# A causal convolution feeding a gated feed-forward layer: weights fetched in six equal slices of 256 columns, their second halves copied in another order, and the first convolution read out by ScalarE alone

## The chip, the cores and the metric

The kernel runs on one core of a Trainium2 chip. The metric is the device time of one execution in microseconds (us). Every line number below is one of the kernel before, as its profile has them, unless the text says otherwise.

## The reference, cut to what matters

```python
# lightweight convolution: x is (8, 4096, 192), weight is (8, 7)
w = softmax(weight, axis=-1)                  # one row of 7 taps per head
x_pad = concat([zeros((8, 6, 192)), x], axis=1)
attn[b, s, 24*h + g] = sum_k w[h, k] * x_pad[b, s + k, 24*h + g]
# gated feed-forward layer over 32768 tokens
t = attn.reshape(32768, 192)
out = (maximum(t @ w_gate, 0) * (t @ w_val)) @ w_out   # 192 -> 1536 -> 192
```

Inputs and output are fp32; the kernel works in fp16 with fp32 sums.

## The kernel before, in words

**Two streams on the two halves of the array.** The eight batches are taken as two streams of four. Channels are cut into three chunks of 64 (`c` = 0 to 2), and partitions 0 to 63 hold a chunk of stream 0, partitions 64 to 127 the same chunk of stream 1. A matrix product of the first layer is therefore issued as pairs of 64-row matmuls on the two row halves of TensorE (L539). This needs each weight matrix twice: `Wg` and `Wv` (gate and value, 192 by 1536) lie in partitions 0 to 63, and again in 64 to 127. DMA brings the first copy, in column slices named by `CUTS` (L156): slice 0 has 128 columns, slices 1 to 4 have 256, slice 5 has 384. An on-chip copy on VectorE or GpSimd makes the second (L168, L177). "f0" to "f11" below are the twelve blocks of 128 columns of the first layer, in the order in which `gate_val` takes them.

**Units.** Sixteen units of 1024 tokens of each stream, `u` = 0 to 15. A unit has two windows of 512. For each window and each f, `gate_val` issues twelve matmuls (gate and value, three chunks, two streams), ScalarE writes the rectified gate (L550, tile `gr`), and VectorE multiplies it by the value out of PSUM (L551, tile `hT`). Then `project` multiplies by `Wo` (L568; L617 at the end), ScalarE and sometimes VectorE copy the result out of PSUM (L594), and SP stores it.

**Where the convolution comes from.** For later units, GpSimd, ScalarE and VectorE compute it beside TensorE, from tiles that GpSimd loads and rearranges (`lane_load` L199, `lane_turn` L463) and SP transposes (L467). At the very start there is no time for that. There, TensorE computes it with band matrices (`conv_dense`, L361): 120 small matmuls for window 0 of unit 0 (`first_block`, before f0) and 120 for window 1 (`second_block`, called between f4 and f5 of window 0). The results go from PSUM into the fp16 tile `xc`, which is the moving operand of L539. In `first_block`, ScalarE copies chunks 0 and 1 and VectorE copies chunk 2 (L379).

**What sets the order of the work.** Nothing is scheduled automatically: each engine runs its instructions in program order, and a semaphore wait holds everything behind it on that engine. GpSimd issues the loads of the first microseconds as well as its copies, all in one order: the first tokens (L125, L126), slices 0, 1 and 2 (each gate, then value), the tokens of window 1 (L87, tile `x_h`, one DMA per stream), slice 3, the copy of slice 2 (gate whole, value in two parts), slice 4, the gate part of slice 5, the copy of slice 3, the value part of slice 5, the copy of slice 4, `Wo` (L695), the copy of slice 5, and then the lane's loads. VectorE copies slice 0 at the beginning of `first_block` and slice 1 behind the chunk that it reads out. PSUM is handed out in four tiles of two banks in rotation. A new pair for f can start only when the pair of f-2 has been read by L550 and L551.

For f0 alone the twelve matmuls run chunk by chunk (gate and value of chunk 0, then of chunk 1, then of chunk 2); every other f takes all of the gate first.

Of the kernel before, what the change touches and what calls it, by code (L numbers as in the profile page):

```python
# [16 lines left out]
def kernel(  # L17
# [12 lines left out]
    nc = tc.nc  # L30
# [4 lines left out]
    DFF = moe_w_gate.shape[1]  # L35
    PAD = KW - 1
    NB = B // 2
    NCH = D // 64
    NBLK = D // 32
    NFF = DFF // 128  # L40
    WIN = 512
# [33 lines left out]
    def load_x(g):  # L75


        bp, toks = GROUPS[g]
        n, rows, step = len(toks), SUB if g < 2 else 128, toks[1] - toks[0]
        xt = xts[g] = xpool.tile([128, GSUB, 2, D], F16, name="x_h")  # L80
        for st in range(2):
            src = bass.AP(
                tensor=x.tensor,
                offset=x.offset + ((bp + NB * st) * S + toks[0] - PAD) * D,
                ap=[[D, rows], [step * D, n], [1, D]],
            )
            nc.gpsimd.dma_start(out=xt[0:rows, 0:n, st, :], in_=src)  # L87
            yield

    def load_rest(steps):  # L90
        for _ in steps:
            pass
# [11 lines left out]
    def stage(p0, rows, st, n_st, jj, n):  # L104
        at = room[p0 : p0 + rows, 0, 0, 0:1]
        dims = [[D * GSUB, n_st], [D, n], [1, D]]
        return bass.AP(
            tensor=at.tensor,
            offset=at.offset + D * (GSUB * st + jj),
            ap=[at.ap[0]] + [d for d in dims if d[1] > 1],  # L110
        )
# [3 lines left out]
    def body(st):  # L115
# [11 lines left out]
        out=xts[0][PAD : PAD + FIRST, 0, :, :],  # L127
        in_=bass.AP(
            tensor=x.tensor, offset=x.offset, ap=[[D, FIRST], [NB * S * D, 2], [1, D]]
        ),  # L130
# [22 lines left out]
    Wg = const.tile([128, NCH, DFF], F16)  # L153
    Wv = const.tile([128, NCH, DFF], F16)
    Wo = const.tile([128, NFF, D], F16)
    CUTS = [0, 128, 384, 640, 896, 1152, DFF]  # L156

    def load_w(s, which=3):
        cols = slice(CUTS[s], CUTS[s + 1])
        for src, dst in ((moe_w_gate, Wg), (moe_w_val, Wv))[which == 2 : 1 + (which > 1)]:  # L160
            nc.gpsimd.dma_start(
                out=dst[0:64, :, cols],
                in_=src.rearrange("(c p) f -> p c f", p=64)[:, :, cols],
            )

    def both_halves(copy, s, dst):
        cols = slice(CUTS[s], CUTS[s + 1])
        copy(out=dst[64:128, :, cols], in_=dst[0:64, :, cols])  # L168

    def pool_halves(s):  # L170
        both_halves(nc.gpsimd.tensor_copy, s, Wg)
        both_halves(nc.gpsimd.tensor_copy, s, Wv)

    def pool_parts(s):
        both_halves(nc.gpsimd.tensor_copy, s, Wg)
        for f0 in range(CUTS[s], CUTS[s + 1], 128):
            nc.gpsimd.tensor_copy(out=Wv[64:128, :, f0 : f0 + 128], in_=Wv[0:64, :, f0 : f0 + 128])  # L177

    xes, xrs, accs, prods = {}, {}, {}, {}

# [6 lines left out]
    def lane_load(v, hold=None):  # L187
# [4 lines left out]
        for j0, n, t in pieces(v):  # L192
# [4 lines left out]
            for st in range(2):  # L197
# [16 lines left out]
                    )  # L214
                yield

    load_w(0)
    load_w(1)
    load_w(2)
    load_rest(load_x(1))  # L220
    load_w(3)
    pool_parts(2)
    load_w(4)
    load_w(5, 1)
    pool_halves(3)
    load_w(5, 2)

    ex = const.tile([H, KW + 1], FP)
    nc.vector.memset(ex[:, KW : KW + 1], 1e-9)
# [21 lines left out]
    with nc.allow_low_precision("zero and one"):  # L251
        nc.vector.tensor_tensor(
            out=same[:], in0=col[:, 0:SEG], in1=s_of[:].to_broadcast([SUB, SEG]), op=ALU.is_equal
        )
        nc.vector.tensor_scalar(
            out=places[:, SUB - SEG : SUB - SEG + NROW],
# [7 lines left out]
        out=mx[:], in_=wr[:], axis=mybir.AxisListType.X, op=ALU.max, negate=True  # L264
# [6 lines left out]
    with nc.allow_low_precision("rounded as the band is"):  # L271
        nc.vector.tensor_scalar(
            out=soft[:],
# [7 lines left out]
        out=spread[0:SUB, 0, 0:H],  # L281
# [7 lines left out]
    with nc.allow_low_precision("products with one and zero"):  # L289
        nc.vector.tensor_tensor(  # L290
            out=diag[:],
# [6 lines left out]
    for a in range(2):  # L298
        for b in range(NSEG):
            nc.tensor.matmul(  # L300
                out=(bps, spread)[a][:, a, HB * SEG * b : HB * SEG * (b + 1)],
# [9 lines left out]
    for cols in (slice(0, 64), slice(64, D)):  # L311
        nc.scalar.copy(
            out=xts[0][0:ROWS0, 1:GSUB, 0, cols],
            in_=stage(0, ROWS0, 0, 1, 1, GSUB - 1)[:, :, cols],
# [25 lines left out]
    xc = {}  # L340
# [3 lines left out]
    def conv_dense(g, c, ps, bank):  # L344


        xt = xts[g]
        toks = GROUPS[g][1]
        t0 = toks[0]
        ends = toks[1:] + [t0 + WIN]  # L350
        for jj in (1, 2, 3, 4, 0):
            col, n = toks[jj] - t0, ends[jj] - toks[jj]
            rows = n + PAD
            for second in range(2):
                for st in range(2):
                    for k2 in range(2):
                        k = 2 * c + k2
                        h0, h1 = 32 * k // G, (32 * k + 31) // G
                        h, m = (h0, G * h1 - 32 * k) if second else (h1, 32)
                        p0 = 64 * st + 32 * k2  # L360
                        nc.tensor.matmul(  # L361
                            out=ps[p0 : p0 + m, bank, col : col + n],
                            lhsT=xt[0:rows, jj, st, 32 * k : 32 * k + m],
                            rhs=band(h)[0:rows, 0:n],
                            start=True,
                            stop=True,
                            tile_position=(0, p0),
                            skip_group_check=True,
                        )

    def first_block():
        xc[0] = xcpool.tile([128, NCH, UNIT], F16, name="xc")
        both_halves(nc.vector.tensor_copy, 0, Wg)
        both_halves(nc.vector.tensor_copy, 0, Wv)
        for c in range(NCH):
            ps = psum.tile([128, 2, 512], FP, name="ps")
            conv_dense(0, c, ps, 0)
            copy = nc.vector.tensor_copy if c == 2 else nc.scalar.copy
            copy(out=xc[0][:, c, 0:WIN], in_=ps[:, 0, :])  # L379

    def second_block():
        two, one = [psum.tile([128, 2, 512], FP, name="ps") for _ in range(2)]
        conv_dense(1, 0, two, 0)
        conv_dense(1, 1, two, 1)
        nc.scalar.copy(out=xc[0][:, 0:2, WIN : 2 * WIN], in_=two[:])
        conv_dense(1, 2, one, 0)
        nc.vector.tensor_copy(out=xc[0][:, 2, WIN : 2 * WIN], in_=one[:, 0, :])
# [138 lines left out]
    def gate_val(u, w):  # L526
        h = hpool.tile([128, NFF, 2, WIN], F16, name="hT")
        xcb = xc[u]
        for f in range(NFF):
            if u == 0 and w == 0 and f == 5:  # L530
                second_block()
            pss = [psum.tile([128, 2, 512], FP, name="ps") for _ in range(2)]
            order = [(i, c) for i in range(2) for c in range(NCH)]
            if u == 0 and w == 0 and f == 0:
                order = [(i, c) for c in range(NCH) for i in range(2)]
            for i, c in order:
                W = (Wg, Wv)[i]
                for st in range(2):
                    nc.tensor.matmul(  # L539
                        out=pss[i][:, st, :],  # L540
                        lhsT=W[64 * st : 64 * st + 64, c, 128 * f : 128 * (f + 1)],
                        rhs=xcb[64 * st : 64 * st + 64, c, WIN * w : WIN * (w + 1)],
                        start=(c == 0),
                        stop=(c == NCH - 1),
                        tile_position=(64 * st, 0),
                    )
            by_stream = u == 0 and w == 0 and f < 2
            for sts in (slice(0, 1), slice(1, 2)) if by_stream else (slice(0, 2),):
                gr = gpool.tile([128, 2, WIN], F16, name="gr")
                nc.scalar.activation(out=gr[:, sts], in_=pss[0][:, sts], func=ACTF.Relu)  # L550
                nc.vector.tensor_tensor(  # L551
                    out=h[:, f, sts], in0=gr[:, sts], in1=pss[1][:, sts], op=ALU.mult
                )
        return h
# [121 lines left out]


    first_block()
    taps = const.tile([H, KW], FP)
    nc.scalar.activation(taps[:], ex[:, 0:KW], ACTF.Copy, scale=sm[:])  # L680
    tap = const.tile([128, NCH, KW], FP)
    for h in range(H):
        r = G * h
        while r < G * (h + 1):
            c, n = r // 64, min(64 - r % 64, G * (h + 1) - r)
            nc.sync.dma_start(
                out=tap[r % 64 : r % 64 + n, c, :],
                in_=taps[h : h + 1, :].unsqueeze(1).to_broadcast([1, n, KW]),
            )
            r += n  # L690

    both_halves(nc.vector.tensor_copy, 1, Wg)
    both_halves(nc.vector.tensor_copy, 1, Wv)
    pool_halves(4)
    nc.gpsimd.dma_start(out=Wo[:], in_=moe_w_out.rearrange("(c p) d -> p c d", p=128))  # L695
    pool_halves(5)
    load_rest(lane_load(1))
    nc.gpsimd.tensor_copy(out=tap[64:128], in_=tap[0:64])
    load_rest(load_x(2))
# [3 lines left out]
    for u in range(NUNIT):  # L703
# [6 lines left out]
        if u == 0:  # L710
            hs.append(gate_val(0, 0))
# [10 lines left out]
        while len(hs) < 2:  # L722
            hs.append(gate_val(u, len(hs)))
# [45 lines left out]
```

## Time and profile before

| | us |
|---|---|
| median of 3 runs | 765.72 (765.51 to 765.99) |
| the profiled execution | 766.03 |
| its span, first to last instruction | 764.2 |
| TensorE busy in the span | 760.4 (99%) |
| VectorE, ScalarE, GpSimd busy | 705.7, 600.3, 378.8 |

How to read it: the profile page gives the busy time of each engine, and a chain of work followed back from the last instruction. Where the chain stays on one engine from end to end, that engine's own length is the time, and only its gaps can be taken away. PE is TensorE's matmuls, PEld its weight loads (which run ahead of the matmul that uses them), DVE is VectorE, ACT is ScalarE, POOL is GpSimd, SP the queue that issues the transposes and stores. In a timeline a row has the start, the time from the first to the last of the merged instructions, the engine, the line, the operation, what it writes and reads, and in brackets how long the engine sat idle before and what ended it. Matmuls of the two row halves overlap, so the time of one says less than the distance from one to the next.

### The profile page before, as it was taken

The page shows a single profiled execution, that of the slowest core. Times are in us where ns is not written, and L with a number is a line of the kernel's source. Part 1 is how long each engine was busy: PE and PEld are TensorE (multiplying, and loading weights), DVE is VectorE, ACT ScalarE, POOL GpSimd, SP SyncE. Part 2 cuts the span into 40 slices and gives each one's busy share as a digit, 9 for nine tenths or more (in the row PEclk, how much of TensorE's full clock was granted, in tenths as well). Part 3 has the DMA queues.
Part 4 walks back from the last instruction along what each step waited for, and adds up shares of the span by engine and source line. Part 5 has one row for each costly group of instructions (what it writes and reads, how often), then busy time and mean ns, then how long its engine had stood idle before and what let it go on. Part 6 is the DMA issues. An engine that isn't in the chain of part 4 may idle for free.

```text
span 764.2 us, 25118 instructions
## 1 busy us (share of the span) xinstructions
PE 760.4 (99%) x10935; PEld 518.6 (68%) x10935; DVE 705.7 (92%) x768; ACT 600.3 (79%) x733; POOL 378.8 (50%) x249
## 2 busy tenths in 40 slices
PE   9999999999999999999999999999999999999998
PEld 4495775957659576585866858567595775957658
DVE  7998999999999999999999999999999999999891
ACT  6787887878878787887878878787887887876571
POOL 8519448093571916629175390853909347090000
PEclk9999999999999999999999999999999999999999
DMA  9969037280442805529162281832818034220202
GB/s 117 130 111 145 7 97 79 65 114 22 95 64 84 95 24 109 46 85 95 32 113 36 85 94 44 107 29 90 88 44 130 8 98 60 64 49 16 70 1 84
DMA packets 131830, 55.93 MB, mean 73 GB/s; under 512 B 96584, under 2 KB 131720, under 8 KB 131720
## 3 DMA queue, kind: packets, MB, share of 16 engines
q1 hardware_dynamic: 90472, 38.66, 23.3%
q0 software_dynamic: 41104, 15.57, 20.6%
q8 instruction: 85, 1.39, 0.8%
q14 instruction: 25, 0.20, 0.1%
q10 hardware_dynamic: 144, 0.10, 0.0%
HBM read 31.48 MB, written 25.17 MB: 74 GB/s over the span
## 4 chain that ended last, share of the span: by engine, by line
PE 99%; ACT 0%; issue 0%
PE ps L539 65%; PE ps L568 32%; PE ps L617 1%; PE ps L145 0%; PE ps L361 0%; PE ps L300 0%; PE ps L402 0%; ACT acc L594 0%; PE ps L280 0%
## 5 line engine op out<-in xcount | busy, mean ns | idle before, releaser
L551 DVE TENSOR_TENSOR hT<-gr,ps 128x1024 f16<-128x1024 f16 (+1 forms) x386 | 469.1, 1216 | 36.2 <-ACT gr L550 9.4
L550 ACT ACTIVATE gr<-ps 128x1024 f16<-128x1024 f32 (+1 forms) x386 | 393.3, 1020 | 102.5 <-PE ps L539 100.6
L489 POOL TENSOR_TENSOR prods<-prods 128x1344 f32<-128x1344 f32 x70 | 212.3, 3032 | 289.8 <-DVE prods L485 286.4
L539 PE MATMUL ps<-xc,Wv 64*128 64x512 f16 x2304 | 316.6, 376 | 0.0
L539 PE MATMUL ps<-xc,Wg 64*128 64x512 f16 x2304 | 316.2, 376 | 0.0
L568 PE MATMUL ps<-Wo,hT 64*128 64x192 f16 x5952 | 248.8, 243 | 0.0
L568 PEld LDWEIGHTS <-hT 64*128 64x128 f16 x5952 | 246.4, 94 | 3.5
L539 PEld LDWEIGHTS <-Wv 64*128 64x128 f16 x2304 | 136.0, 94 | 113.4 <-POOL Wv L177 0.4
L539 PEld LDWEIGHTS <-Wg 64*128 64x128 f16 x2304 | 123.7, 94 | 121.4 <-issue 0.4
L513 DVE SCALAR_TENSOR_TENSOR acc<-x_r,tap,acc 128x576 f32<-128x576 f16 x225 | 165.3, 811 | 0.0
L483 ACT ACTIVATE prods<-x_r,tap 128x448 f32<-128x448 f16 x222 | 130.0, 660 | 0.0
L594 ACT COPY out_s<-ps 128x768 f32<-128x768 f32 (+1 forms) x64 | 45.6, 713 | 51.2 <-PE ps L568 39.8
L199 POOL DMA_DIRECT2D x_e<-in_x_dram x58 | 47.0, 822 | 15.3 <-ACT acc L499 11.5
L463 POOL COPY x_p<-x_e 128x960 f16<-128x960 f16 (+1 forms) x58 | 50.3, 907 | 0.7 <-DMA x_e<-in_x_dram 0.7
L489 POOL TENSOR_TENSOR xc<-prods 128x1344 f16<-128x1344 f32 x14 | 42.4, 3030 | 1.1
L513 DVE SCALAR_TENSOR_TENSOR xc<-x_r,tap,acc 128x576 f16<-128x576 f16 x45 | 34.1, 811 | 0.0
L499 ACT ACTIVATE acc<-x_r,tap 128x576 f32<-128x576 f16 x45 | 31.4, 763 | 0.0
L485 DVE TENSOR_SCALAR prods<-x_r,tap 128x448 f32<-128x448 f16 x70 | 26.6, 448 | 0.0
L594 DVE COPY out_s<-ps 128x384 f32<-128x384 f32 (+1 forms) x16 | 8.6, 540 | 11.5 <-PE ps L617 9.4
L617 PE MATMUL ps<-Wo,hT 128*128 128x192 f16 x96 | 8.1, 246 | 0.0
L617 PEld LDWEIGHTS <-hT 128*128 128x128 f16 x96 | 7.9, 98 | 0.2 <-issue 0.2
L145 PE MATMUL ps<-const-bfloat16-1.0 128*128 128x512 bf16 (+1 forms) x8 | 3.8, 609 | 0.8 <-PEq L753 0.8
(56 smaller groups left out, 55.9 us busy)
## 6 DMA issues: line engine op xcount, KB each, us to landing
out_dram<-out_s SPq DMA_DIRECT2D x62, 384.0 KB, 2.7
x_e<-in_x_dram POOLq DMA_DIRECT2D x34, 192.0 KB, 7.5
x_e<-in_x_dram POOLq DMA_DIRECT2D x24, 240.0 KB, 5.0
x_r<-x_p SPq DMA_TRANSPOSE x131, 4.7
Wo<-in_moe_w_out_dram POOLq DMA_DIRECT2D x1, 576.0 KB, 6.6
x_h<-in_x_dram POOLq DMA_DIRECT2D x2, 210.0 KB, 6.1
Wg<-in_moe_w_gate_dram POOLq DMA_DIRECT2D x4, 96.0 KB, 4.8
Wv<-in_moe_w_val_dram POOLq DMA_DIRECT2D x4, 96.0 KB, 5.8
```

The lines of the kernel that those rows point to most:

```text
L199: first = nc.gpsimd.dma_start(out=xe[:, j0 + start : j0 + n, st, :, :].rearrange("p j c r -> p j (c r)"), in_=bass.AP(tensor=x.tensor, off ...
L463: nc.gpsimd.tensor_copy(out=xp[:, j0 : j0 + n, :, st, :], in_=xe[:, j0 : j0 + n, st, :, :])
L483: engine.activation(out=out, in_=in_, func=ACTF.Copy, scale=scale)
L485: engine.tensor_scalar(out=out, in0=in_, scalar1=scale, scalar2=None, op0=ALU.mult)
L489: nc.gpsimd.tensor_tensor(out=pr[:, 0] if k < KW - 1 else xc[v + 1][:, :, LDVE:UNIT], in0=pr[:, 0], in1=pr[:, k], op=ALU.add,)
L499: nc.scalar.activation(out=accs[v][:, c, :], in_=shifted(v, c, 0, 0), func=ACTF.Copy, scale=tap[:, c, 0:1],)
L513: nc.vector.scalar_tensor_tensor(out=xc[v][:, c, 0:LDVE] if k == KW - 1 else acc[:, c, :], in0=shifted(v, c, k, 0), scalar=tap[:, c, k : k ...
L539: nc.tensor.matmul(out=pss[i][:, st, :], lhsT=W[64 * st : 64 * st + 64, c, 128 * f : 128 * (f + 1)], rhs=xcb[64 * st : 64 * st + 64, c, WI ...
L550: nc.scalar.activation(out=gr[:, sts], in_=pss[0][:, sts], func=ACTF.Relu)
L551: nc.vector.tensor_tensor(out=h[:, f, sts], in0=gr[:, sts], in1=pss[1][:, sts], op=ALU.mult)
L568: mm = nc.tensor.matmul(out=outs[q], lhsT=h[64 * r : 64 * r + 64, f, st, 128 * q : 128 * (q + 1)], rhs=Wo[64 * r : 64 * r + 64, f, :], sta ...
L594: one(out=dst[:, step * j : step * j + step], in_=src[:, step * j : step * j + step])
```

## The change

The weights come in six slices of 256 columns, so that slice s holds the blocks f(2s) and f(2s+1). VectorE copies the second halves of f0 (before the first convolution's results are read) and of f1 (behind that); GpSimd copies all the others. GpSimd's order becomes: the first tokens, slices 0, 1 and 2, the tokens of window 1, the copy of f2 and f3 in one piece for gate and one for value, slice 3, the copies of f4 and then of f5 (gate and value of each), slices 4 and 5, and then the copies of f6 and f7, of f8 and f9, of f10 and f11, and only then `Wo`. In `first_block`, ScalarE copies all three chunks. The order of f0's matmuls becomes: gate of chunks 0 and 1, value of chunks 0 and 1, gate of chunk 2, value of chunk 2. Nothing else is touched; the products and their number are the same.

```diff
-    CUTS = [0, 128, 384, 640, 896, 1152, DFF]
-
-    def load_w(s, which=3):
-        cols = slice(CUTS[s], CUTS[s + 1])
-        for src, dst in ((moe_w_gate, Wg), (moe_w_val, Wv))[which == 2 : 1 + (which > 1)]:
+    PAIR = 256
+
+    def load_w(s):
+        cols = slice(PAIR * s, PAIR * (s + 1))
+        for src, dst in ((moe_w_gate, Wg), (moe_w_val, Wv)):
             nc.gpsimd.dma_start(
...
-    def both_halves(copy, s, dst):
-        cols = slice(CUTS[s], CUTS[s + 1])
-        copy(out=dst[64:128, :, cols], in_=dst[0:64, :, cols])
...
+    def both_halves(copy, f0, n=1):
+        cols = slice(128 * f0, 128 * (f0 + n))
+        for dst in (Wg, Wv):
+            copy(out=dst[64:128, :, cols], in_=dst[0:64, :, cols])
...
-    load_w(0)
-    load_w(1)
-    load_w(2)
+    for s in range(3):
+        load_w(s)
     load_rest(load_x(1))
+    both_halves(nc.gpsimd.tensor_copy, 2, 2)
     load_w(3)
-    pool_parts(2)
+    both_halves(nc.gpsimd.tensor_copy, 4)
+    both_halves(nc.gpsimd.tensor_copy, 5)
     load_w(4)
-    load_w(5, 1)
-    pool_halves(3)
-    load_w(5, 2)
+    load_w(5)
...
-        both_halves(nc.vector.tensor_copy, 0, Wg)
-        both_halves(nc.vector.tensor_copy, 0, Wv)
+        both_halves(nc.vector.tensor_copy, 0)
         for c in range(NCH):
             ps = psum.tile([128, 2, 512], FP, name="ps")
             conv_dense(0, c, ps, 0)
-            copy = nc.vector.tensor_copy if c == 2 else nc.scalar.copy
-            copy(out=xc[0][:, c, 0:WIN], in_=ps[:, 0, :])
+            nc.scalar.copy(out=xc[0][:, c, 0:WIN], in_=ps[:, 0, :])
...
             if u == 0 and w == 0 and f == 0:
-                order = [(i, c) for c in range(NCH) for i in range(2)]
+                order = [(0, 0), (0, 1), (1, 0), (1, 1), (0, 2), (1, 2)]
...
-    both_halves(nc.vector.tensor_copy, 1, Wg)
-    both_halves(nc.vector.tensor_copy, 1, Wv)
-    pool_halves(4)
+    both_halves(nc.vector.tensor_copy, 1)
+    for f0 in (6, 8, 10):
+        both_halves(nc.gpsimd.tensor_copy, f0, 2)
     nc.gpsimd.dma_start(out=Wo[:], in_=moe_w_out.rearrange("(c p) d -> p c d", p=128))
-    pool_halves(5)
     load_rest(lane_load(1))
```

More of the change, by code (lines that the diff above doesn't have):

```diff
@@ L164, in load_w @@
             )
-    def both_halves(copy, s, dst):
-        cols = slice(CUTS[s], CUTS[s + 1])
[L168 to L177, printed above, removed]
+    def both_halves(copy, f0, n=1):
+        cols = slice(128 * f0, 128 * (f0 + n))
+        for dst in (Wg, Wv):
+            copy(out=dst[64:128, :, cols], in_=dst[0:64, :, cols])
     xes, xrs, accs, prods = {}, {}, {}, {}
```

## The prediction, made before the run

> **What bounds the kernel now.** I read the page's chain first. It is TensorE from end to end, so what counts is the length of that engine's work and its gaps. Then the chain in order of time (start, length, what) shows where the gaps can be.
>
> ```profile
> PE ps L539 65%; PE ps L568 32%; PE ps L617 1%; PE ps L145 0%; PE ps L361 0%; PE ps L300 0%; PE ps L402 0%; ACT acc L594 0%; PE ps L280 0%
> ...
> 7.22 5.19 PE ps L539 x43
> 12.41 0.03 issue
> 12.44 2.11 PE ps L539 x17
> 14.55 1.48 PE ps L361 x120
> 16.03 24.71 PE ps L539 x228
> ...
> 57.25 31.08 PE ps L539 x288
> ```
>
> In a later unit 288 matmuls of L539 take 31.08 us, or 0.1079 each; twelve (one f) take 1.295. From 16.03 the 228 matmuls take 24.71, or 0.1084 each: nothing to win behind 16.03. Before that, f0 to f4 (43 + 17 = 60 matmuls) take from 7.22 to 14.55, 7.33 us, where 60 x 0.1079 = 6.47 would do. **So 0.86 us is lost in the whole stage that the change touches**, and that is the ceiling of any gain: 0.11% of 766. A measurement of this kernel can tell about 0.2% (1.5 us) from no change. A gain of that size would have to come from where the trace shows no gap.
>
> Where are the 0.86 us? The timeline of the weight loads names each stop, in brackets, and that of the matmuls shows what it cost:
>
> ```profile
> 7.61 0.09 PEld L539 LDWEIGHTS <-Wv 64*128 64x128 f16 x1 [0.35 <-DVE Wv L168]
> ...
> 8.33 0.09 PEld L539 LDWEIGHTS <-Wg 64*128 64x128 f16 x1 [0.39 <-issue]
> ...
> 12.43 0.33 PEld L539 LDWEIGHTS <-Wv 64*128 64x128 f16 x5 [0.36 <-POOL Wv L177]
> ...
> 8.76 0.84 PE L539 MATMUL ps<-xc,Wg 64*128 64x512 f16 x6
> ...
> 12.04 1.22 PE L539 MATMUL ps<-xc,Wv 64*128 64x512 f16 x6
> ```
>
> The loads run a little ahead of the matmuls, so a bracket overstates the loss. f1's matmuls begin at 8.76. From 7.22, f0 thus takes 1.54 instead of 1.295: 0.25 lost, on the copy of Wv (7.61) and on the third chunk (8.33). The six value matmuls of f3 take 1.22 from the first to the last where f1's gate ones take 0.84: some 0.40 lost on POOL's copy of the value weights (12.43). The rest, 0.21, is short waits and the passage into the second convolution; I count on 0.08 of it.
>
> **The change, part by part.** *f0.* The rows of DVE and ACT:
>
> ```profile
> 6.55 0.28 DVE L168 COPY Wg<-Wg 64x384 f16<-64x384 f16 x1 [0.64 <-DMA Wg<-in_moe_w_gate_dram]
> 7.11 0.45 DVE L168 COPY Wv<-Wv 64x384 f16<-64x384 f16 x1 [0.27 <-DMA Wv<-in_moe_w_val_dram]
> 7.59 0.69 DVE L379 CAST xc<-ps 128x512 f16<-128x512 f32 x1
> 8.31 0.42 DVE L168 COPY Wg<-Wg 64x768 f16<-64x768 f16 x1
> 8.65 0.55 DVE L168 COPY Wv<-Wv 64x768 f16<-64x768 f16 x1
> ...
> 6.36 1.07 ACT L379 CAST xc<-ps 128x512 f16<-128x512 f32 x2 [0.65 <-PE ps L361]
> 7.32 0.29 ACT L680 ACTIVATE taps<-ex,sm 8x7 f32<-8x7 f32 x1
> ```
>
> ACT takes two chunks in 1.07, the second 0.48 behind the first. The third starts at 7.32, where taps stands now, and ends at about 7.90; DVE's ends at 8.28. `xc` is whole 0.38 earlier. taps and the ten small DMAs behind it on SP move by 0.5; GpSimd reads what they bring only at 24.79 (row below), so that costs nothing.
>
> Against this, slice 0 grows from 128 to 256 columns, so its two DMAs carry 96 KB each instead of 48. Time to landing, from the DMA view of short stretches, in the order of issue (the first two in the 48 KB form):
>
> ```profile
> Wg<-in_moe_w_gate_dram POOLq DMA_DIRECT2D x1, 48.0 KB, 3.5
> Wv<-in_moe_w_val_dram POOLq DMA_DIRECT2D x1, 48.0 KB, 3.5
> ...
> Wg<-in_moe_w_gate_dram POOLq DMA_DIRECT2D x1, 96.0 KB, 3.6
> Wv<-in_moe_w_val_dram POOLq DMA_DIRECT2D x1, 96.0 KB, 5.8
> ...
> x_h<-in_x_dram POOLq DMA_DIRECT2D x1, 210.0 KB, 6.1
> ...
> Wg<-in_moe_w_gate_dram POOLq DMA_DIRECT2D x1, 96.0 KB, 5.9
> ```
>
> Gate of slice 2, at 96 KB, took 3.6, hardly more than the 48 KB ones. The bounds for the two new DMAs are thus 0 and, by the 5.8, +2.3. I take +0.1 for gate and +0.2 for value, near the row of the same size with the same predecessors. Value lands at 7.3 instead of 7.1, its copy (0.28 to 0.45 by the two rows) ends at 7.6 to 7.8, and the rest of f0 behind it, 8 matmuls at 0.108, ends at 8.5 to 8.7. I take 8.64: gain 0.12. DVE copies f1 directly behind, in at most 2 x 0.45, by 8.6; f1's value is wanted at 9.3.
>
> *f2 and f3* become POOL's. The rows of POOL that give its pace:
>
> ```profile
> 4.82 0.63 POOL L161 DMA_DIRECT2D Wv<-in_moe_w_val_dram  x1
> ...
> 6.68 1.63 POOL L87 DMA_DIRECT2D x_h<-in_x_dram  x2
> 8.30 0.65 POOL L161 DMA_DIRECT2D Wg<-in_moe_w_gate_dram  x1
> ...
> 11.88 0.95 POOL L177 COPY Wv<-Wv 64x384 f16<-64x384 f16 x2 [1.45 <-DMA Wv<-in_moe_w_val_dram]
> ...
> 14.65 0.84 POOL L168 COPY Wg<-Wg 64x768 f16<-64x768 f16 x1
> 15.41 0.84 POOL L168 COPY Wv<-Wv 64x768 f16<-64x768 f16 x1
> ...
> 18.34 1.08 POOL L695 DMA_DIRECT2D Wo<-in_moe_w_out_dram  x1
> ...
> 21.60 0.88 POOL L199 DMA_DIRECT2D x_e<-in_x_dram  x1
> ...
> 24.79 0.24 POOL L698 COPY tap<-tap 64x21 f32<-64x21 f32 x1
> ```
>
> A 256-column copy follows the one before by 0.77, a 128-column copy by 0.475 (0.95 for two), and a weight DMA takes 0.63. Up to 8.30 POOL's list has the same length. From there, now in the new order: gate of f2/f3 at 8.30, value at 9.07 to 9.9 (slice 1 was there for DVE at 8.31 and 8.65, at most 0.1 to 0.3 later now). f2 begins at 8.64 + 1.295 = 9.94 and wants its value weights at 10.6: covered by 0.7. Slice 3 is issued 9.84 to 11.09. Gate of f4 at 11.09. Its value must wait for slice 2's value DMA, which by the 5.8 lands at 11.85. The time of its issue, some 6.06, is the 4.82 and two more issues of 0.62. That wait stands in the trace now (1.45 idle at 11.88); it shrinks to about 0.3 because POOL has other things to do first. Value of f4 at 11.9, f5 at 12.37 and 12.85, end 13.32. f4 begins at 8.64 + 3 x 1.295 = 12.53 and wants its value weights at 13.2: covered by 0.8. **So the 0.40 of f3 is gone**, and the short waits with it.
>
> f4 ends at 13.82, and *the second convolution* starts at about 13.87 instead of 14.48, if its tokens are there. The later x_h DMA is issued at about 7.5 and takes 6.1: it lands at 13.6 to 13.7, as now. Covered by 0.2. It ends at 15.38, f6 begins at 16.68 and wants its value weights at 17.32; before it had them at 17.92:
>
> ```profile
> 14.48 1.55 PE L361 MATMUL ps<-band,x_h 110*32 110x104 f16 x120
> ...
> 17.92 0.81 PE L539 MATMUL ps<-xc,Wv 64*128 64x512 f16 x6
> ```
>
> So TensorE alone would be 0.60 earlier. *What is late next* is POOL: four DMA issues (4 x 0.63 = 2.52) now stand between the copy of f5 and that of f6. Issued from 13.32 to 15.83; gate of f6/f7 copied 15.83 to 16.66 (f6 wants it at 16.68: a tie), value 16.60 to 17.43, seen by TensorE 0.05 later, at 17.48. TensorE waits 0.16. **The sum is 17.92 - 17.48 = 0.44 us gained.** Slice 3's landing (9.84 + 5.9 = 15.7) just precedes its copy.
>
> *Behind that.* f8/f9 are copied 17.4 to 19.0, f10/f11 18.9 to 20.4, for use from 19.4 and from 22. `Wo` is issued at about 20.4 instead of 18.34 and takes 6.6 to land; its first use is at 40.58:
>
> ```profile
> Wo<-in_moe_w_out_dram POOLq DMA_DIRECT2D x1, 576.0 KB, 6.6
> ...
> 40.58 0.66 PE L568 MATMUL ps<-Wo,hT 64*128 64x192 f16 x12
> ...
> 47.22 0.80 ACT L594 COPY out_s<-ps 128x768 f32<-128x768 f32 x1 [0.54 <-PE ps L568]
> ```
>
> 13 us of cover. The lane's loads start at 21.5 instead of 21.60: the two wide copies (1.16 us each in the old order) become two pairs of 0.77, POOL has two copies more, and the idle 1.45 pays for them. The lane is no later in absolute time, but TensorE reaches it 0.44 earlier; ACT, which serves both, still idles 0.54 for TensorE at 47.22, so I cost this at nothing; without that cover it could take back the 0.44.
>
> The profiled execution took 766.03, 1.8 more than its span. 766.03 - 0.44 = 765.59. The median of the runs is 0.31 below the profiled one, so the forecast for the median is 765.72 - 0.44 = **765.3 us**.
>
> **The rivals.**
> *POOL is not late* (765.1). If slice 2's value lands after about 3.7 as gate did, not 5.8, POOL loses no 0.3 at f4, and f6 is copied by 17.1: the gain is TensorE's own 0.60. For it: three of the first four quoted took 3.5 to 3.6. Against it: the late one had this very place. In its flight stands one 16 KB instruction fetch, which from 8.2 to 10.5 took 5.8% of 16 engines, so one engine for 2.1 us:
>
> ```profile
> q8 instruction: 1, 0.02, 5.8%
> ```
>
> Nothing in the change moves TensorE's program up to there.
>
> *DVE and POOL get in each other's way* (765.5). The copy of Wv at 7.11 took 0.45, that of Wg, of the same shape, 0.28. If that is a wait for the other engine, it will happen again where DVE's copies of f1 (now 7.8 to 8.5) meet POOL's DMA issues and its first copy at 8.30. POOL's list then starts 0.2 later, its spare 0.3 at f4 takes part of it, and POOL's copy of f6 or f0's end costs 0.1 to 0.3. For it: 0.45 against 0.28. Against it: POOL's own issues beside DVE's copies at 8.31 and 8.65 took 0.65, like all others. The Trainium skill (SBUF — State Buffer, section Who interferes with whom) has this as a rule: VectorE's copies can take a port pair that GpSimd needs, and the other "fully blocks". By that rule alone the sum would be near +0.2; in the trace only DVE shows a delay, not POOL, so the rule decides one of my cases and not the forecast.
>
> *Slower: the late DMA moves forward* (766.4). POOL's list now has value of f2/f3 ahead of everything. If slice 1's value, issued at 4.82, is the DMA that is held up, as slice 2's is now (5.8 instead of 3.6), it lands at 10.6. The copy ends at 11.45, f2 stands still for 0.85, and all later issues and copies move by 1.5: value of f6 is there at 17.48 + (10.6 - 9.07) less the 0.3 spare, 18.6, which is 0.7 after 17.92. It costs more than the change gains from the point at which this DMA takes more than about 5.0. For it: the DMAs quoted from slice 2's value on took 5.8 to 6.1, and slices 0 and 1 carry 96 KB more before it. Against it: slice 1's value has been there by 8.65 until now.
>
> *It doesn't remove the stall but moves it* (765.7). If x_h lands 0.6 later, TensorE waits in front of the second convolution instead: nothing gained. Its DMAs stand behind 96 KB more, at 0.6 per 96 KB issued, and POOL issues them no later: 0 to 0.3 later is what I would expect.
>
> **How the numbers follow.** Forecast (gain 0.3 to 0.5): 0.40. POOL not late: 0.18. Port or slow copies (gain 0.1 to 0.3): 0.18. Stall moved (within 0.1 of now): 0.09. Slower, 0.2 to 0.9: 0.11; worse than 1.5, if both slices' late landings add up: 0.03. Something unseen faster: 0.01. The range runs from the best case, 765.1 less the spread of 0.3 among runs, to 766.3, in the slower case: 764.8 to 766.3 leaves out some 0.15. By the bound of 0.2%, nearly all cases are "the same": faster 0.01, same 0.95, slower 0.04.
>
> **What would show it.** In the profile after: the gap in front of f3's value loads gone; POOL's idle time in front of f4's value copy under 0.5; the second convolution at 13.9 (14.5 means that x_h is late); a short stop of TensorE in front of f6's value weights, released by POOL, at about 17.5; chunk 2 read out by ACT by 7.9 and f1 from about 8.6; `Wo` at 20.4 and the lane's first load at 21.5; everything behind 40 as before, 0.4 earlier. Wrong would be a TensorE gap behind 20, a value DMA of slice 1 landing after 9.1, or a difference over 0.9 us in either direction.

## The result, and the profile after

The changed kernel takes 768.36 us (median of 22 runs, 767.14 to 774.24), the kernel before 765.85 beside it (22 runs, 765.50 to 771.62). The ratio is 1.0044, with a 95% interval of 1.0027 to 1.006. The forecast was 765.3 and the range ended at 766.3: the change is slower, by 2.5 us in the median, and its times spread over 7 us, where 20 of 22 runs of the kernel before lie within 1.7. The ratio, here and below, counts the rare long runs of both kernels, so that it can lie below 1 where the medians say otherwise. From here on "lane" is the convolution beside TensorE, "x_e" its loads, "x_r" its transposed tokens.

The profiled execution took 773.6 (span 771.5), so it shows the loss near its largest. Twelve of the 22 spans lie from 765.1 to 766.3 and ten from 767.9 to 772.2; of the shorter kind there is no trace, and how its loss divides is known only from the experiments. Line numbers of the changed kernel are 8 to 11 lower behind the first 160 lines: L528 is L539 of before, L557 is L568, L456 the transposes and L472 ScalarE's lane products (L467 and L483 of before) and L191 the loads of x_e (L199). This is its chain in order of time (start, length, what); in the kernel before it was PE up to the last read-out.

```profile
2.30 3.98 DMA x_h<-in_x_dram
...
6.32 1.22 PE ps L352 x85
7.54 6.78 PE ps L528 x60
14.32 1.48 PE ps L352 x119
15.80 5.95 PE ps L528 x54
...
22.64 7.72 DMA x_e<-in_x_dram
...
42.45 2.02 SPq L456
...
44.52 6.49 DMA x_r<-x_p
...
51.11 2.90 ACT prods L472 x5
54.02 0.74 ACT y L416 x2
...
54.80 9.75 PE ps L557 x192
64.55 31.08 PE ps L528 x288
```

Read it from the end. From 64.55 on all is as before: 31.08 us for a gate stage. The first 16 us went the way that was forecast, but by less: the 60 matmuls of f0 to f4 take 6.78 instead of 7.33, and the second convolution begins at 14.32 instead of 14.55 in this view, although f0 begins 0.32 late. That is 0.23 gained there, where 0.6 was forecast. Between these 16 us and 64.55 stands a piece that no step of the prediction has: a load of x_e of 7.72 us, nine transposes, ScalarE, and only then TensorE again. The timeline of TensorE gives the two gaps:

```profile
45.98 0.51 PE L391 MATMUL ps<-x_h,band 64*128 64x192 f16 x8 [1.31 <-SPq L404]
...
54.80 1.47 PE L557 MATMUL ps<-Wo,hT 64*128 64x192 f16 x18 [4.19 <-ACT y L416]
```

The first, 1.31, waits for a marker on SP's queue (L404, "first turn over") that stands behind the transposes there. The second, 4.19, waits for a PSUM tile that ScalarE has yet to read out, and ScalarE sits in front of its lane products until the last transposes land. The view of waits (who for whom, us in total, times, longest) gives that:

```profile
ACT prods L472 <- DMA x_r<-x_p: 8.0, 1, 8.0
```

The gap costs more than itself. This is the view by stretches, which ends with the granted clock, the DMA share and GB/s: first the stretch behind the gap, then an undisturbed projection.

```profile
54.80:64.55 9.75, 9.75 (x194) 9.68 (x195) 2.34 (x6) 7.98 (x15) 6.96 (x6) 0.82 0.28 89
95.63:111.47 15.84, 15.84 (x387) 15.78 (x384) 15.77 (x24) 13.77 (x23) 0.00 (x0) 1.00 0.19 57
```

At a granted clock of 0.82, 192 matmuls of L557 take 9.75 us; at 1.00, 384 take 15.84, so 192 would take 7.92. That is another 1.83. 1.31 + 4.19 + 1.83 = 7.33. Since TensorE had come to this stage 0.22 earlier than before (the first L557 at 40.36, the first L568 at 40.58), 7.11 of the 7.3 by which the spans differ is accounted for; 0.2 stays open.

Where it begins is POOL's timeline of the changed kernel:

```profile
20.70 1.08 POOL L684 DMA_DIRECT2D Wo<-in_moe_w_out_dram  x1
21.77 3.23 POOL L191 DMA_DIRECT2D x_e<-in_x_dram  x4
...
29.08 0.98 POOL L452 COPY x_p<-x_e 128x960 f16<-128x960 f16 x1 [2.19 <-DMA x_e<-in_x_dram]
```

and of the kernel before:

```profile
26.66 1.90 POOL L463 COPY x_p<-x_e 128x960 f16<-128x960 f16 x2
```

The loads are issued at 21.77, as before (21.60), and Wo at 20.70 as forecast (20.4). But the copies that need x_e begin at 29.08 instead of 26.66. The DMA view of this stretch has the reason, before and then after (KB each, median us from issue to landing):

```profile
x_e<-in_x_dram POOLq DMA_DIRECT2D x2, 240.0 KB, 4.8
x_e<-in_x_dram POOLq DMA_DIRECT2D x2, 192.0 KB, 5.5
```

```profile
x_e<-in_x_dram POOLq DMA_DIRECT2D x2, 240.0 KB, 7.5
x_e<-in_x_dram POOLq DMA_DIRECT2D x2, 192.0 KB, 7.9
```

Wo's 576 KB now stand 1.07 us ahead of x_e in GpSimd's DMA queue; before they stood 3.26 ahead, with the two wide copies between. So x_e takes 2.4 to 2.7 longer from issue to landing, and the nine transposes (the next rows, before and after) start 2.8 later.

```profile
28.59 13.05 SPq L467 DMA_TRANSPOSE x_r<-x_p  x9
```

```profile
31.42 14.36 SPq L456 DMA_TRANSPOSE x_r<-x_p  x9
```

Their issue ends at 45.78 instead of 41.64, and so they meet the lane's second loads, which ScalarE's first product releases at 42.31 (42.38 before):

```profile
42.31 3.19 POOL L191 DMA_DIRECT2D x_e<-in_x_dram  x4 [9.06 <-ACT acc L488]
```

The last transposes, with these loads beside them, need 6.49 us to land (the chain above) and come at 51.0. In the kernel before the last two needed 2.5. That the loads are what slows them is shown by number 4 below.

### The profile page after: what moved, and what is told of

It reads as the page before. It is cut to its first block, busy times and chain, and to the rows that moved or that the text cites. A ratio compares the mean times of both kernels' runs of the same rounds, so it can differ in the third digit from the quotient of the medians.

```text
span 771.5 us, 25121 instructions
## 1 busy us (share of the span) xinstructions
PE 761.3 (99%) x10935; PEld 527.5 (68%) x10935; DVE 704.2 (91%) x767; ACT 600.4 (78%) x734; POOL 380.0 (49%) x252
## 4 chain that ended last, share of the span: by engine, by line
PE 95%; DMA 2%; SPq 2%; ACT 1%; POOL 0%; issue 0%; POOLq 0%; ACTq 0%
PE ps L528 62%; PE ps L557 31%; SPq L456 2%; PE ps L606 1%; DMA x_e<-in_x_dram 1%; DMA x_r<-x_p 1%; DMA x_h<-in_x_dram 1%; ACT prods L472 0%; PE ps L352 0%; POOL x_p L452 0%; POOL x_h L125 0%; POOL x_e L191 0%; ACT y L416 0%; ACT acc L583 0%; POOL steps L124 0%
## 5 line engine op out<-in xcount | busy, mean ns | idle before, releaser
L539 ACT ACTIVATE gr<-ps 128x1024 f16<-128x1024 f32 (+1 forms) x386 | 392.9, 1019 | 101.7 <-PE ps L528 99.8
L528 PE MATMUL ps<-xc,Wg 64*128 64x512 f16 x2304 | 317.5, 377 | 0.0
L528 PE MATMUL ps<-xc,Wv 64*128 64x512 f16 x2304 | 317.3, 376 | 0.0
L557 PE MATMUL ps<-Wo,hT 64*128 64x192 f16 x5952 | 250.7, 244 | 4.2 <-ACT y L416 4.2
L557 PEld LDWEIGHTS <-hT 64*128 64x128 f16 x5952 | 248.2, 95 | 7.7 <-issue 4.3
L528 PEld LDWEIGHTS <-Wv 64*128 64x128 f16 x2304 | 138.5, 94 | 110.2 <-issue 0.4
L528 PEld LDWEIGHTS <-Wg 64*128 64x128 f16 x2304 | 128.5, 94 | 116.4 <-issue 0.2
L472 ACT ACTIVATE prods<-x_r,tap 128x448 f32<-128x448 f16 x222 | 130.1, 661 | 8.0 <-DMA x_r<-x_p 8.0
L191 POOL DMA_DIRECT2D x_e<-in_x_dram x58 | 47.0, 822 | 12.8 <-ACT acc L488 9.1
L169 POOL COPY Wv<-Wv 64x768 f16<-64x768 f16 (+1 forms) x6 | 4.3, 720 | 0.5 <-DMA Wv<-in_moe_w_val_dram 0.4
```

What stands on the lines that cost most here:

```text
L191: first = nc.gpsimd.dma_start(out=xe[:, j0 + start : j0 + n, st, :, :].rearrange("p j c r -> p j (c r)"), in_=bass.AP(tensor=x.tensor, off ...
L472: engine.activation(out=out, in_=in_, func=ACTF.Copy, scale=scale)
L528: nc.tensor.matmul(out=pss[i][:, st, :], lhsT=W[64 * st : 64 * st + 64, c, 128 * f : 128 * (f + 1)], rhs=xcb[64 * st : 64 * st + 64, c, WI ...
L557: mm = nc.tensor.matmul(out=outs[q], lhsT=h[64 * r : 64 * r + 64, f, st, 128 * q : 128 * (q + 1)], rhs=Wo[64 * r : 64 * r + 64, f, :], sta ...
```

## The experiments

Theory A: Wo directly ahead of x_e makes the lane late, and the late transposes then collide with the second loads. Rival B: the loss comes from the new slices and copies, through GpSimd or the traffic of the first 20 us. Each run below is given with its median, range and number of runs, and the median of the kernel before beside it.

**1. Wo ahead of the last copies.** In the changed kernel:

```diff
-    for f0 in (6, 8, 10):
+    for f0 in (6, 8):
         both_halves(nc.gpsimd.tensor_copy, f0, 2)
     nc.gpsimd.dma_start(out=Wo[:], ...)
+    both_halves(nc.gpsimd.tensor_copy, 10, 2)
     load_rest(lane_load(1))
```

> The changed kernel with one edit: Wo is issued ahead of the copy of f10 and f11 instead of behind it, some 1.5 us earlier. Theory A (Wo's 576 KB stand directly ahead of the lane's loads in GpSimd's DMA queue, so x_e lands 2.8 us late, the transposes start late, and TensorE waits between 44 and 55): x_e lands within about 1 us of where it does in the kernel before, the two long TensorE gaps are gone or under 0.5 us, and the time is 765.3 to 766.2, so between 0.5 us faster and 0.4 slower than before. Theory B (the loss comes from the new slices and copies themselves, through GpSimd or the DMA traffic of the first 20 us): the time stays near 768.4.

766.59 (766.07 to 768.21, 12 runs) against 765.75; ratio 0.9998 (0.9974 to 1.0023). Neither gap is left, and 1.8 of the 2.5 us are. B is refuted for the main part; A missed the rest: 0.8 over the kernel before, where at most 0.4 was expected.

**2. Wo behind the copies in the kernel before**, and nothing else:

```diff
-    nc.gpsimd.dma_start(out=Wo[:], ...)
     pool_halves(5)
+    nc.gpsimd.dma_start(out=Wo[:], ...)
     load_rest(lane_load(1))
```

> The kernel before with one edit: Wo is issued behind the copy of the last slice, directly ahead of the lane's loads. Nothing else of the change. Theory A: Wo at 20.7 instead of 18.3, x_e landing 2 to 3 us later, gaps of TensorE between 44 and 55, time 767.5 to 770, with a spread of several us from run to run as the changed kernel has. Theory B: 765.8 as before, since Wo is wanted only at 40.

770.94 (767.75 to 774.10, 10 runs) against 765.75; ratio 1.0051 (1.0021 to 1.008). This line alone makes the whole loss and more, also more than the 767.5 to 770 that A expected; why it costs twice what it costs in the changed kernel is open. Its waits between 38 and 60 show the second of the changed kernel's two gaps; the first, behind SP's marker, is not there:

```profile
ACT prods L483 <- DMA x_r<-x_p: 5.1, 1, 5.1
...
PE ps L568 <- ACT y L427: 2.6, 1, 2.6
```

**3. The lane's loads ahead of Wo** in the changed kernel:

```diff
-    nc.gpsimd.dma_start(out=Wo[:], ...)
     load_rest(lane_load(1))
+    nc.gpsimd.dma_start(out=Wo[:], ...)
```

> The changed kernel with one edit: the lane's four loads are issued ahead of Wo, which follows them. Theory A: x_e lands about 1 us earlier than in the kernel before, no TensorE gap behind 20, and what is left is the gain of the first 18 us alone, 765.2 to 765.6 (0.2 to 0.6 us under before). Wo lands by 35, in time for 40. Theory B: near 768.4, and if Wo came late TensorE would wait at 40.

766.45 (766.03 to 768.05, 12 runs) against 765.75; ratio 0.9994 (0.9971 to 1.0017). The gaps are gone again, and Wo is in time. But the "gain of the first 18 us" did not come: 0.7 over before, not 0.4 under. Its chain:

```profile
2.31 3.88 DMA x_h<-in_x_dram
6.23 1.22 PE ps L352 x88
7.45 6.78 PE ps L528 x60
14.23 1.48 PE ps L352 x120
15.71 24.73 PE ps L528 x228
```

Here the first convolution waits for the second DMA of the first tokens (72 KB, L126), and f0 begins at 7.45, not 7.22. The stop in front of f6 that the prediction put at 0.16 is not there: from 15.71 the 228 matmuls take 24.73, before 24.71.

**4. The second loads held** until the last transposes have landed, in the changed kernel:

```diff
-            load_rest(lane_load(2, begun))
+            load_rest(lane_load(2, turned[1]))   # turned[v]: the last transpose of lane v
```

> The changed kernel with one edit: the lane's second set of loads waits for the last transposes of the first instead of for ScalarE's first lane product. Theory A with a collision (the lateness alone costs 1 to 2 us, and the rest and the spread come from the last transposes sharing the DMA engines with the second loads): the last transposes land by 46 to 47 instead of 51, ScalarE waits about 3 us instead of 8, the time is 766.3 to 767.3 with a spread under 1 us. Theory A without a collision (lateness alone): 768 and the same spread. Theory B: no change from 768.4.

766.71 (765.98 to 767.95, 10 runs) against 765.75; ratio 0.9991 (0.9962 to 1.002). Wo still stands ahead of x_e and x_e still lands late (7.1 to 7.6 us after issue). Yet without the collision the lateness costs almost nothing:

```profile
ACT prods L472 <- DMA x_r<-x_p: 2.2, 1, 2.2
```

ScalarE waits 2.2 instead of 8.0, and TensorE does not wait. The last transpose lands 3.7 us after its issue, and ScalarE's products begin at 45.55 instead of 51.11. So most of the price is that of the collision, and the lateness is only what leads to it. It was expected at 766.3 to 767.3 with a spread under 1 us; the spread is 2.

**5. to 8. The other 0.7 us.** Theory C: the doubled first slice, queued right behind the first tokens, makes their second DMA late. Theory D: it has another source. Number 5 is number 3 with slices of 128, 384 and four times 256 columns; 6 is the kernel before with `CUTS = [0, 256, 384, ...]` and VectorE's copies in their old shapes; 7 is the kernel before with these two edits of the change; 8 is the kernel before with the lane's loads ahead of Wo.

```diff
+        nc.scalar.copy(out=xc[0][:, c, 0:WIN], in_=ps[:, 0, :])                       # 7
+        order = [(0, 0), (0, 1), (1, 0), (1, 1), (0, 2), (1, 2)]                      # 7
```

> The changed kernel with the lane's loads ahead of Wo (as in the run before this one) and with slices of 128, 384 and four times 256 columns, so that the first slice is 48 KB again; the copies stay as they are. Theory C (the doubled first slice, queued right behind the first tokens, makes the second DMA of these tokens land 0.3 to 0.7 us later, and the first convolution waits for it): that DMA lands 3.6 us after its issue instead of 3.9 to 4.4, f0 begins at 7.1 to 7.3, and the median is 0.3 to 0.6 us under the 766.45 of the run with six equal slices. Theory D (the 0.7 us by which that run is over the kernel before have another source, ScalarE's read-out, the copies or the order): the median stays within 0.2 of 766.45.

> The kernel before with the first slice 256 columns wide and the second 128; VectorE's copies keep their shapes (128 columns, then 256). Theory C: the second DMA of the first tokens lands 3.9 us or more after its issue instead of 3.6, f0 begins at 7.4 or later, and the median is 0.3 to 0.6 over before. Theory D: within 0.2 of before.

> The kernel before with two parts of the change alone: ScalarE reads out the third chunk, and f0's matmuls go in the new order. By the prediction's step f0 takes 0.1 to 0.2 us less, so the median is 0.0 to 0.2 under before. Theory D (these parts cost something): over before by 0.2 or more, in the span or outside of it.

> The kernel before with Wo issued behind the lane's first loads. Theory A: x_e lands 1 us or more earlier than in the kernel before, nothing waits for Wo, median 765.5 to 765.8. If the few runs of the kernel before at 770 to 773 come from the same collision of the last transposes with the second loads, they should be rarer or gone here, since the transposes end earlier.

Against 765.74: number 5 took 766.29 (765.93 to 767.66, 11 runs; ratio 1.0, 0.9984 to 1.0017), number 6 took 766.81 (765.76 to 767.71, 11 runs; 1.001, 1.0001 to 1.0019), number 7 took 766.05 (765.82 to 767.73, 11 runs; 1.0004, 0.9995 to 1.0013), number 8 took 765.82 (765.52 to 766.12, 11 runs; 0.9992, 0.9972 to 1.0013).

Number 6 bears out C in the direction, at twice the size: with the wide first slice the median is 1.07 higher. Its token DMA took 4.3 us, against 3.7 in the kernel before:

```profile
x_h<-in_x_dram POOLq DMA_DIRECT2D x1, 72.0 KB, 4.3
```

But the lateness explains only 0.6 of it. This execution's span is 765.7, and its first convolution also ran at the slower of two speeds (last section), which alone is 0.84. So 1.07 is not the price of the late DMA by itself, and whether the slow speed comes from the wide slice is not shown.

Number 5 came out as D expected: the median is 0.16 under that of number 3, and f0 begins at 7.47. It does not refute C, since the DMA that C is about was late there too (3.9): the first slice is small again, but a slice of 144 KB follows. So C stays unproven. Number 8 is the kernel before within 0.1: x_e was issued 1.15 us earlier, but GpSimd came to its copies at 26.59, no sooner than before (26.66). Number 7 is the surprise, and D's outcome. ScalarE's read-out and the order gain nothing, and cost 0.31; its median span is that of the kernel before (763.9), and what lies outside the span is 2.09 instead of 1.83.

**9. and 10. The two parts of number 7 apart**, each alone in the kernel before.

> The kernel before with f0's new matmul order alone. The run with the order and ScalarE's read-out together was 0.31 over before, all of it outside the span (2.09 us there instead of 1.82). If the order makes it: 2.09 outside the span here, median 766.0. If ScalarE's additional instruction makes it: 1.82 outside, median 765.7 to 765.8.

> The kernel before with ScalarE's read-out of the third chunk alone. If ScalarE's additional instruction makes the 0.26 us outside the span: 2.09 outside, median 766.0. If the order makes it: 1.82 outside, median 765.7.

Against 765.88: the order alone 765.79 (765.57 to 774.03, 10 runs; ratio 1.0011, 0.9986 to 1.0036), with 1.82 outside the span; ScalarE's read-out alone 766.24 (765.57 to 772.64, 10 runs; 1.0011, 0.999 to 1.0031), with 2.09 outside. It goes with ScalarE's read-out, which gives that engine one instruction more (734 on the page, 733 before). What it is outside the span, no view shows: open.

The profiled execution of number 10 is of use for another thing. It has before's order of Wo, and Wo happened to take 8.7 us to land there, with this wait behind it (L482 is L483 of before):

```profile
ACT prods L482 <- DMA x_r<-x_p: 2.8, 1, 2.8
```

So the kernel before stands near the same edge. That its rare long runs are those in which it goes over is not shown, since there is no trace of one.

**11. Half of Wo ahead, half behind**, in the changed kernel: 288 KB before the copy of f10 and f11 and 288 KB directly ahead of the lane's loads.

> The changed kernel with Wo in two DMAs of 288 KB, the first ahead of the copy of f10 and f11, the second behind it, so that half as much stands directly ahead of the lane's loads. Theory A: x_e lands between the two cases (second load at about 29 us instead of 27.8 and 30.4), and the time lies between the 766.6 of all of Wo ahead and the 768.4 of all behind: 766.7 to 767.8, with some runs over 769 if the collision has a threshold.

767.66 (766.38 to 773.88, 10 runs) against 765.88; ratio 1.0023 (0.9998 to 1.0048). Between the two ends, as expected, and by the spread it is the edge: seven spans lie from 764.3 to 766.2, three from 769.1 to 771.8.

**12. The kernel before with the lane's loads ahead of Wo and the second loads held.**

> The kernel before with two edits: Wo behind the lane's first loads, and the second loads held until the last transposes have landed. Theory A: the collision that makes the rare runs of 770 to 774 in the kernel before cannot happen any more; median 765.6 to 765.9, and no run over 767.5. If those rare runs have another cause, one or two of some eleven would still be over 768 (7 of 68 of the kernel before are).

765.80 (765.48 to 767.20, 12 runs) against 765.88; ratio 0.9996 (0.9983 to 1.0009). No run's median is more than 0.1 under that of the kernel before beside it. But none of the 46 runs with the lane's loads first (numbers 3, 5, 8, 12) took over 769, and of the 125 runs of the kernel before beside the changed kernel and the twelve experiments 11 did. That fits A; a rate of 11 in 125 would by chance still give none of 46 about once in seventy times. Of the edits that leave Wo where it was, numbers 6 and 7 had none in 22 and numbers 9 and 10 three in 20.

## Why the prediction was wrong

**The step that failed** is the last of the parts, under "Behind that": "The lane's loads start at 21.5 instead of 21.60 ... The lane is no later in absolute time", and "so I cost this at nothing". The start was right (21.77) and the conclusion was not: a TensorE gap behind 20, which the prediction named as a sign of being wrong, is what came. For Wo I counted the 13 us until its own first use, and for x_e the time of its issue. I did not count what Wo does to the DMAs behind it in its queue, though the rows were there: Wo takes 6.6 to land, x_e 4.8 to 5.5, and 3.26 us lay between the two issues. The two issues moved together by 3.26 - 1.07 = 2.2, and x_e landed 2.4 to 2.7 later: about that much, and a little more. 2.8 us of lateness alone would have been a small loss (number 4); the price came from a second meeting, with the loads that ScalarE releases at 42.3. The cover that I named, ScalarE's 0.54 of idle time at 47.22, was that of an engine behind the transposes, not the margin of the transposes themselves.

None of my rivals was this. The slower one (slice 1's value late) did not happen: that DMA took 4.4 us, under the 5.0 from which it would have decided. (Its sum, 17.48 + 1.53 - 0.3, is 18.7 and not 18.6, which changes nothing.) The range was built from cases in the first 18 us, and so was too narrow on the one side where I had looked least.

**Right in mechanism, wrong in size or in base.**
- *The ceiling of 0.86.* In the profiled executions the 60 matmuls of f0 to f4 took 6.78 with the new slices and copies (numbers 1, 3 and 4 and the changed kernel alike). With the old ones they took 7.33 in the one that I had, but 6.85 in number 2, 6.95 in number 7, 6.70 in number 9, 6.61 in number 12. The 5.8 us landing of slice 2 that stopped f3 does not come every time (4.2 in number 2). I read a single execution's wait as a standing cost, although that execution was 0.31 over the median.
- *f0.* ScalarE had chunk 2 out at 8.20, not 7.90, but before TensorE came to it (8.41); f0's weights came 0.3 (gate) and 0.24 (value) later, where 0.1 and 0.2 were forecast. f0 itself took 1.31 (7.54 to 8.85) instead of 1.54, so this part of the mechanism was right. What I had not bounded is the DMA *ahead* of the grown slice: the tokens' second DMA took 4.0 (3.9 to 4.4 in numbers 1, 3 and 4), not 3.7, and it holds the first convolution. f0 began at 7.45 to 7.93 instead of 7.22, which took back 0.2 to 0.7.
- *POOL as the next limit.* POOL was not late at f6: its copy of the value weights ended at 17.21 (forecast 17.43), and TensorE came to them at 17.69 (forecast 17.32). Slice 2's value landed after 4.3 us and cost POOL no wait.
- *The second convolution* at 14.2 to 14.7 (forecast 13.87): late by what f0 is late, and by 0.13 because f0 to f4 took 6.78 where the forecast had 6.65.
- *The port rival.* VectorE's copies of f0 and f1 took 0.27 to 0.29 each in the changed kernel (0.33 at most in number 3); the 0.45 of the kernel before did not come again, though GpSimd was issuing DMAs at the time. The rule of the Trainium skill that I weighed there (SBUF — State Buffer, Who interferes with whom) decided nothing in these runs.

The 2.5 us of the medians thus are: 1.9 by Wo's place (768.36 to 766.45 in number 3), 0.5 of span that number 3 keeps (a median of 764.4 against 763.9), and 0.27 outside the span with ScalarE's read-out; these add up to 2.7, within the differences among the sets of runs. The 0.5 should lie in the first 16 us or so: in every profiled execution without a gap behind 20, the time from the end of the second convolution (15.55 to 17.52) to the end of the span is 748.1 to 748.3. Which step there makes it is not shown; number 3's own profiled execution, with a span of 763.9, does not have it.

## What to carry to other kernels

When a transfer is moved, look not only for its first use but for whatever is issued behind it in its queue: a load that is wanted late can still be in the way of one that is wanted early. Then follow the delayed work to the next transfer that some other engine starts at its own time, because two streams that just miss each other now may meet after the move. And before a wait is booked as a gain, ask whether it is there in every execution; a profiled run above the median is a warning.

## What the runs showed of the hardware

**A gap lowers the clock behind it.** After the 4.19 us gap the granted clock of TensorE was 0.82 over the next 9.75 us, and the gap cost another 1.83. The Trainium skill (TensorE: Matmul & The Clock Gate, Part 1) has the rule that the array's clock follows how busy it was in windows of about 3.4 us, and falls to half after at least one idle window; this trace agrees, with its gap of 4.19. Number 2 does not: its gap of 2.64 is shorter than such a window, and still the granted clock was 0.83 over the 9.76 us behind it, with 0.50 from 53 to 55 us. The measurement decides: here 2.64 us was enough, while behind the changed kernel's gap of 1.31 the clock stayed at 1.00. The price did not follow the length of the gap either: behind the 3.48 us gap of number 11 the same 192 matmuls took 10.77 us (clock 0.74), behind 2.64 and 4.19 us 9.75.

**The first convolution runs at two speeds.** In the profiled execution of number 6, the 88 matmuls behind the tokens' wait took 2.06 us and a pair of f0's 0.61; in number 4, 1.22 and 0.39 for matmuls of the same shapes. First the timeline of number 6 (L364 and L542 there are L361 and L539 of before), then that of number 4 (L352 and L528):

```profile
6.62 2.06 PE L364 MATMUL ps<-band,x_h 102*32 102x96 f16 x88 [0.52 <-DMA x_h<-in_x_dram]
8.61 0.61 PE L542 MATMUL ps<-xc,Wg 64*128 64x512 f16 x2
```

```profile
6.71 1.22 PE L352 MATMUL ps<-band,x_h 102*32 102x96 f16 x88 [0.64 <-DMA x_h<-in_x_dram]
...
8.81 0.39 PE L528 MATMUL ps<-xc,Wg 64*128 64x512 f16 x2
```

The granted clock reads 1.00 in both stretches, so this column does not show it; only the durations do. Five of number 6's eleven spans are 765.5 or more, while the rest lie from 763.9 to 765.0; whether these five are the slow form throughout is not shown, since only one of them has a trace.

**Tokens in front of larger DMAs landed later.** The 72 KB of tokens were issued 0.67 us before the first slice and landed 3.5 to 3.8 us after issue in front of 48 KB slices (the kernel before, numbers 2, 7 to 10 and 12) and 3.9 to 4.4 in front of 96 KB ones (the changed kernel, numbers 1, 3, 4, 6 and 11). In number 5, where 48 KB slices follow the tokens and 144 KB ones come behind these, they took 3.9. The cause is open.
